# Two-stage attention with a gated convolution: groups of 508 tokens with their own halo, h summed on VectorE, outputs partly from float16 halves

## The chip, the cores and the metric

The kernel runs on one core of one Trainium2 chip. The metric is the time of one execution on the device, in microseconds (us). The kernel before took 354.98 us, the median of three runs (354.09 to 355.49). The profile comes from one further execution of the same kernel.

## What is computed

There are 4 batches of 12800 tokens with 128 channels, and 32 inducing vectors. In short:

```python
def mab(q, kv):                        # attention with kv as keys and as values
    s = scale * (q @ kv.transpose(0, 2, 1))
    a = np.exp(s - s.max(-1, keepdims=True))
    a /= a.sum(-1, keepdims=True) + 1e-09
    return a @ kv
h = mab(I, x)                          # 32 rows per batch: the inducing vectors attend to all tokens
y = mab(x, h)                          # every token attends to the 32 rows of h
# then, on y, a gate from a causal convolution over 5 tokens, per channel:
gate = 1 / (1 + np.exp(-sum(conv_w[k] * y_padded[:, k:k + S, :] for k in range(5))))
out = (gate * (y @ w_val)) @ w_out
```

The host transposes: the kernel gets x twice, as `xT` (batch, 128 channels, tokens) and as `xk` (batch, 128 rows, blocks, 128 channels), and writes the output transposed.

## The kernel before

Each batch is cut into seven units. Six are big: four groups (G = 4) of 512 tokens, one group for each quarter of the 128 partitions in the attention steps. One is small, four groups of 128 tokens; it stands first in batch 0 and last in the others (`units`, L29).

**Stage 1** makes h. For each unit `load_t` (L218) brings xT, 128 rows of 8192 bytes for a big unit, and `load_k` (L223) brings xk, which is the same tokens again with the token on the partition: 128 rows of 16 blocks of 512 bytes. Both are issued on SyncE's queue (SP), in the order xT, xk, xT, xk. `a_mm` (L229) makes the scores, `a_max` and `a_exp` (L238, L242) the exponentials, `a_tr` (L248) transposes them in blocks of 128 tokens on TensorE, `a_ev` (L254) copies them to SBUF, `a_h` (L259) multiplies them with xk, and `a_hev` (L268) copies the unit's sum. `a_h` is the only reader of xk.

**Between the stages**, once per batch, the `p_` functions (L274 to L381) join the units: `p_F` (L304) makes seven scaled diagonal matrices, `p_h` (L316) sums the seven units with seven float32 matmuls, `p_hq` (L323) normalizes h, and `p_v`, `p_w`, `p_wt`, `p_we` fold h into the weights of the convolution and of `w_val`, as pairs of float16 numbers (a high part and a rest).

**Stage 2** goes over the same units with the xT that is still in SBUF. `b_mm` to `b_back` (L384 to L426) make the attention weights of each token, `b_hi` (L429) and `b_lo` (L434) split them into two float16 halves; `b_lo` also copies, on GpSimd (POOL), the four tokens before each group, the halo, from the group or the unit in front. `c_gate` (L456) runs the five taps as 60 matmuls of 32 rows into four PSUM banks (tag `g`), `c_tanh` (L461) reads them, `c_val` (L466) fills a new tile of the same four banks, `c_gv` (L470) multiplies the two, `c_out` (L475) multiplies one group with `w_out` in float32, `c_ev` (L480) copies the result to SBUF, and after the fourth group the output leaves by a DMA on ScalarE's queue.

**The order** is made by a planner that runs while the program is built (`Plan`, L53). Every step is a task with an engine, a cost, a key (its due time, in units of stage 2), the tasks that it needs and the buffer that it takes. The planner plays the tasks through; of those that can start, an engine takes the one with the lowest key. The order of start becomes the order of the instructions on every engine, and the engines then keep to it. Stage 1 of batch b + 1 has keys in the middle of stage 2 of batch b, so both stages run side by side except in batch 0's stage 1 and in batch 3's stage 2.

Buffers limit how far ahead loads run: 12 for xT (held from the load to `b_mm` in stage 2), 4 for xk (held to `a_h`); the eight PSUM banks are `g` 4, `o` 2, `s` 1, `x` 1 (L38). The host builds `xk` in `kernel` (L607 to L612).

Of the kernel before, what the change touches and what calls it, by code (L numbers as in the profile page):

```python
# [24 lines left out]
SP = 16384.0  # L25
TINY = 1e-30


def units(b):  # L29
    small = [(0, 128)] if b == 0 else [(12288, 128)]  # L30
    big = [(2048 * u + 512 * (b == 0), 512) for u in range(6)]
    return small + big if b == 0 else big + small

# [4 lines left out]
BUFS = dict(xT=12, xk=4, E=2, ET=2, q=3, m=2, z=2, p=2, hl=3, gt=4, os=2, hs=1, nm=3, wst=2, wst2=2, gsc=2, hq=2, s=1, x=1, o=2, g=1)  # L38
LAT = 0.15
SLACK = 0.1  # L40
OUTK = 1.4
KA, KB, KP, KS = -2.5, 0.6, 4.0, 1.3
# [9 lines left out]

class Plan:  # L53
# [5 lines left out]
    def add(self, eng, dur, key, fn, args=(), deps=(), alloc=None, uses=(), lat=LAT):  # L59
        t = dict(i=len(self.tasks), eng=eng, dur=dur, key=key, fn=fn, args=args, deps=set(deps) | set(uses), alloc=alloc,  # L60
                 users=[], lat=lat, start=None, end=None)
# [71 lines left out]
def tile_kernel(ctx: ExitStack, tc: tile.TileContext, xT, xk, inducing, w_val, conv_w, w_out, out):  # L133
# [21 lines left out]
    def constants():  # L155
# [10 lines left out]
        V.memset(ones, 1.0)  # L166
        id4 = const.tile([P, M], F32, name="id4")
# [50 lines left out]
    def load_t(b, u):  # L218
        t0, w = units(b)[u]
        x = st[b, u, "xT"] = sbt("xT", [P, G * 512])  # L220
        nc.sync.dma_start(x[:, :G * w], xT[b, :, t0:t0 + G * w])

    def load_k(b, u):  # L223
        t0, w = units(b)[u]
        n = G * w // P
        x = st[b, u, "xk"] = sbt("xk", [P, 16, P])
        nc.sync.dma_start(x[:, :n, :], xk[b, :, t0 // P:t0 // P + n, :])

    def a_mm(b, u):  # L229
# [5 lines left out]
        for g in range(G):  # L235
            T.matmul(sc[M * g:M * g + M, :w], c_["iw"], x[:, w * g:w * g + w], start=True, stop=True, tile_position=(0, M * g))  # L236
# [11 lines left out]
    def a_tr(b, u):  # L248
        w = units(b)[u][1]
        et = st[b, u, "etp"] = ps("et", "x", [P, 4, P])  # L250
        for i in range(w // P):
            T.transpose(et[:, i, :], st[b, u, "E"][:, P * i:P * i + P], c_["identf"])  # L252

    def a_ev(b, u):  # L254
        n = units(b)[u][1] // P
        et = st[b, u, "et"] = sbt("ET", [P, 4, P])
        S.copy(et[:, :n, :], st[b, u, "etp"][:, :n, :])  # L257

    def a_h(b, u):  # L259
        n = units(b)[u][1] // P  # L260
        hp = st[b, u, "h"] = ps("h", "x", [P, 512])
        et, x = st[b, u, "et"], st[b, u, "xk"]
        for i in range(n):
            for g in range(G):
                T.matmul(hp[M * g:M * g + M, :P], et[:, i, M * g:M * g + M], x[:, n * g + i, :],  # L265
# [38 lines left out]
    def p_F(b):  # L304
        d = bat[b]
        f = d["f"]
        F = d["F"] = sbt("F", [P, NU, M])
        V.tensor_tensor(F, c_["id4"].rearrange("p (o q) -> p o q", o=1).broadcast_to([P, NU, M]), f.broadcast_to([P, NU, M]), ALU.mult)
# [6 lines left out]

    def p_h(b):  # L316
# [3 lines left out]
        for u in range(NU):  # L320
            T.matmul(t[:, :M], d["hs"][:, u, :], d["F"][:, u, :], start=u == 0, stop=u == NU - 1)  # L321
# [16 lines left out]
    def p_w(b):  # L338
# [10 lines left out]
        V.tensor_scalar(vmx, vmx, TINY, 1.0 / SW, ALU.max, ALU.mult)  # L349
# [16 lines left out]
        wo = d["wo"] = sbt("wo", [P, P], tag="wst")  # L366
        V.tensor_scalar(wo, c_["w2"], vmx, 0.5 / SP, ALU.mult, ALU.mult)

# [15 lines left out]
    def b_mm(b, u):  # L384
# [3 lines left out]
        for g in range(G):  # L388
            T.matmul(sc[M * g:M * g + M, :w], bat[b]["hq"], x[:, w * g:w * g + w], start=True, stop=True, tile_position=(0, M * g))  # L389

    def b_tr(b, u):
        w = units(b)[u][1]
# [3 lines left out]
    def b_max(b, u):  # L396
        n = units(b)[u][1] // M
# [3 lines left out]
    def b_sub(b, u):  # L401
        n = units(b)[u][1] // M
# [3 lines left out]
    def b_exp(b, u):  # L406
        n = units(b)[u][1] // M
# [3 lines left out]
    def b_sum(b, u):  # L411
        n = units(b)[u][1] // M
        z = st[b, u, "z"] = sbt("z", [P, 16, 1])
        V.tensor_reduce(z[:, :n, 0], st[b, u, "q"][:, :n, :], AX.X, ALU.add)
        V.tensor_scalar(z[:, :n], z[:, :n], 1e-9, 1.0 / SP, ALU.add, ALU.mult)
        V.reciprocal(z[:, :n], z[:, :n])  # L416

    def b_norm(b, u):
        n = units(b)[u][1] // M
# [3 lines left out]
    def b_back(b, u):  # L423
        w = units(b)[u][1]
# [4 lines left out]
    def b_hi(b, u):  # L429
        w = units(b)[u][1]  # L430
        h = st[b, u, "hl"] = sbt("hl", [P, 2, 520], F16)
        S.copy(h[:, 0, 4:4 + w], st[b, u, "p"][:, :w])  # L432

    def b_lo(b, u):  # L434
        w = units(b)[u][1]
        h = st[b, u, "hl"]
        Gp.tensor_tensor(h[:, 1, 4:4 + w], st[b, u, "p"][:, :w], h[:, 0, 4:4 + w], ALU.subtract)  # L437
        if u == 0:
            Gp.memset(h[:M, :, 0:4], 0.0)
        else:  # L440
# [6 lines left out]
    def strips(b, u, bank, d, k, first, last):  # L447
        w = units(b)[u][1]
        h, wst = st[b, u, "hl"], bat[b]["wst"]
        for i, (part, wp) in enumerate(((0, 0), (0, 1), (1, 0))):  # L450
            for g in range(G):
                s = slice(M * g, M * g + M)
                T.matmul(bank[:, g, :w], wst[s, wp, k, :], h[s, part, 4 - d:4 - d + w],  # L453
# [12 lines left out]
    def c_val(b, u):  # L466
        bank = st[b, u, "v"] = ps("v", "g", [P, G, 512])
        strips(b, u, bank, 0, TAPS, True, True)

    def c_gv(b, u, i):  # L470
        w = units(b)[u][1]
        t = st[b, u, i, "t"]
        V.scalar_tensor_tensor(t[:, :, :w], t[:, :, :w], 1.0, st[b, u, "v"][:, 2 * i:2 * i + 2, :w], ALU.add, ALU.mult)  # L473

    def c_out(b, u, g):  # L475
        w = units(b)[u][1]
        op = st[b, u, g, "o"] = ps("o", "o", [P, 512])
        T.matmul(op[:, :w], bat[b]["wo"], st[b, u, g // 2, "t"][:, g % 2, :w], start=True, stop=True)  # L478

    def c_ev(b, u, g):  # L480
# [4 lines left out]
        S.copy(os[:, w * g:w * g + w], st[b, u, g, "o"][:, :w])  # L485
# [16 lines left out]
    hl = {}  # L502
    hq = [None] * B
    ph = []
    wready = [None] * B

# [120 lines left out]
```

## Time and profile before

| | us |
|---|---|
| median of three runs | 354.98 |
| profiled execution, its own time | 354.44 |
| its span, first to last instruction | 352.7 |
| TensorE matmuls busy in it | 315.0 |
| VectorE busy | 197.9 |
| ScalarE busy | 176.0 |
| GpSimd busy | 103.3 |

The span lies 1.74 us below the execution's own time. Engines: PE is TensorE's matmuls and PEld its weight loads, DVE is VectorE, ACT ScalarE, POOL GpSimd, SP SyncE; a q behind a name is the engine's sequencer or queue. The profile's page shows the span in 40 slices, a digit for the busy tenths of each; the views of groups show a line of the kernel, the engine, the operation, output<-input with shapes, the count, and then the busy time, the mean length of one, and the idle time just before with what ended it.

### The profile page before, as it was taken

The numbers are of one execution on the slowest core, as the hardware profiler recorded it, in microseconds if no ns is written. First come the engines' busy times: TensorE is split into PE (matmuls) and PEld (weight loads), VectorE is DVE, ScalarE is ACT, GpSimd is POOL, SyncE is SP. The second block draws the span as 40 slices with busy tenths as digits, with TensorE's granted clock in tenths as the row PEclk, the third lists the DMA queues.
The fourth block names the chain that finished last, engine by engine and source line by source line (L and its number), as shares of the span: only waits on it lengthen the run. The fifth ranks groups of instructions, "written<-read, shape, count | busy, mean of one in ns | idle before, by whom it ended". The sixth has DMA issues, their size and how long they took to land.

```text
span 352.7 us, 8776 instructions
## 1 busy us (share of the span) xinstructions
PE 315.0 (89%) x3722; PEld 139.3 (39%) x3722; DVE 197.9 (56%) x415; ACT 176.0 (50%) x314; POOL 103.3 (29%) x202
## 2 busy tenths in 40 slices
PE   2475698989999999999999999999999999887774
PEld 0333455543343454343353444443354333332332
DVE  1432356656579773664678563666667758722220
ACT  1223313556553647466553557465654555624443
POOL 0000003434531443144431123443451457721000
PEclk9989959999999999999999999999999999989999
DMA  7999999838983293698983394012223230232233
GB/s 306 419 419 413 419 415 421 315 159 326 388 360 121 70 391 120 227 336 302 414 354 123 106 390 164 32 62 103 93 106 122 121 124 26 119 121 121 119 121 150
DMA packets 12481, 79.49 MB, mean 225 GB/s; under 512 B 1397, under 2 KB 1690, under 8 KB 3226
## 3 DMA queue, kind: packets, MB, share of 16 engines
q1 hardware_dynamic: 8064, 52.43, 38.2%
q10 hardware_dynamic: 4378, 26.50, 18.4%
q8 instruction: 29, 0.48, 0.6%
q14 instruction: 10, 0.08, 0.1%
HBM read 52.71 MB, written 26.21 MB: 224 GB/s over the span
## 4 chain that ended last, share of the span: by engine, by line
PE 79%; ACT 7%; DMA 7%; DVE 5%; issue 1%; ACTq 0%; SPq 0%; DVEq 0%
PE o L478 25%; PE g L453 24%; PE s L389 7%; PE s L236 6%; PE h L265 6%; PE v L453 4%; DMA xT<-in_xt_dram 4%; PE et L252 3%; ACT gt L464 3%; DMA raw<-in_moe_w_out_dram 3%; DVE gt L473 2%; PE t L321 2%; ACT os L485 2%; ACT E L246 1%; DVE nm L240 1%
## 5 line engine op out<-in xcount | busy, mean ns | idle before, releaser
L478 PE MATMUL o<-gt,wo 128*128 128x512 f32 (+1 forms) x224 | 105.0, 584 | 9.1 <-DVE gt L473 8.5
L453 PE MATMUL g<-hl,wstk 32*128 32x512 f16 (+1 forms) x1680 | 86.3, 352 | 0.0
L485 ACT COPY os<-o 128x512 f32<-128x512 f32 (+1 forms) x112 | 58.9, 542 | 50.6 <-PE o L478 49.9
L473 DVE SCALAR_TENSOR_TENSOR gt<-gt,v 128x1024 f32<-128x1024 f32 (+1 forms) x56 | 59.5, 1103 | 41.8 <-ACT os L485 30.1
L453 PEld LDWEIGHTS <-wstk 32*128 32x128 f16 x2016 | 44.7, 92 | 75.2 <-issue 19.3
L464 ACT ACTIVATE gt<-g,gsc 128x1024 f32<-128x1024 f32 (+1 forms) x56 | 54.4, 1019 | 35.0 <-PE g L453 26.8
L478 PEld LDWEIGHTS o<-gt,wo 128*128 128x128 f32 x224 | 36.1, 190 | 53.0 <-issue 32.7
L404 POOL TENSOR_TENSOR q<-q,m 128x512 f32<-128x512 f32 (+1 forms) x28 | 26.7, 955 | 103.2 <-DVE m L399 102.3
L421 POOL TENSOR_TENSOR q<-q,z 128x512 f32<-128x512 f32 (+1 forms) x28 | 26.7, 954 | 70.0 <-DVE z L416 50.6
L437 POOL TENSOR_TENSOR hl<-p,hl 128x512 f16<-128x512 f32 (+1 forms) x28 | 29.6, 1057 | 39.0 <-ACT hl L432 38.8
L246 ACT ACTIVATE E<-s,nm 128x512 f32<-128x512 f32 (+1 forms) x28 | 18.0, 643 | 34.8 <-DVE nm L240 27.1
L265 PE MATMUL h<-xk,ET 128*32 128x128 f32 x800 | 29.7, 289 | 2.5 <-ACT ET L257 2.5
L236 PE MATMUL s<-xT,iw 128*32 128x512 f32 (+1 forms) x224 | 30.7, 624 | 0.6 <-DMA xT<-in_xt_dram 0.3
L240 DVE TENSOR_REDUCE nm<-s 128x1 f32<-128x512 f32 (+1 forms) x28 | 17.6, 630 | 24.3 <-PE s L236 24.1
L265 PEld LDWEIGHTS h<-xk,ET 128*32 128x32 f32 x800 | 23.0, 117 | 17.6 <-ACT ET L257 10.6
L252 PE MATMUL et<-identf,E 128*128 128x128 f32 x100 | 18.1, 303 | 12.8 <-ACT E L246 12.0
L432 ACT CAST hl<-p 128x512 f16<-128x512 f32 (+1 forms) x28 | 16.1, 575 | 26.4 <-DVE p L426 25.1
L389 PE MATMUL s<-xT,hq 128*32 128x512 f32 (+1 forms) x224 | 27.6, 562 | 1.0 <-DVE q L394 1.0
L394 DVE STREAM_TRANSPOSE q<-s 128x512 f32<-128x512 f32 (+1 forms) x28 | 18.1, 645 | 13.3 <-PE s L389 13.2
L426 DVE STREAM_TRANSPOSE p<-q 128x512 f32<-128x512 f32 (+1 forms) x28 | 17.9, 646 | 11.9 <-POOL q L421 10.7
L453 PE MATMUL v<-hl,wstk 32*128 32x512 f16 (+1 forms) x336 | 21.2, 354 | 1.9 <-ACT gt L464 1.9
L409 ACT ACTIVATE q<-q 128x512 f32<-128x512 f32 (+1 forms) x28 | 16.4, 589 | 13.0 <-POOL q L404 12.5
(85 smaller groups left out, 194.8 us busy)
## 6 DMA issues: line engine op xcount, KB each, us to landing
xT<-in_xt_dram SPq DMA_DIRECT2D x24, 1024.0 KB, 9.5
xk<-in_xk_dram SPq DMA_DIRECT2D x24, 1024.0 KB, 11.4
out_dram<-os ACTq DMA_DIRECT2D x24, 1024.0 KB, 4.5
xT<-in_xt_dram SPq DMA_DIRECT2D x4, 256.0 KB, 8.7
xk<-in_xk_dram SPq DMA_DIRECT2D x4, 256.0 KB, 6.3
out_dram<-os ACTq DMA_DIRECT2D x4, 256.0 KB, 2.0
raw<-in_moe_w_val_dram ACTq DMA_DIRECT2D x1, 128.0 KB, 7.6
raw<-in_moe_w_out_dram ACTq DMA_DIRECT2D x1, 128.0 KB, 10.1
```

The costliest lines, as they stand in the source:

```text
L236: T.matmul(sc[M * g:M * g + M, :w], c_["iw"], x[:, w * g:w * g + w], start=True, stop=True, tile_position=(0, M * g))
L252: T.transpose(et[:, i, :], st[b, u, "E"][:, P * i:P * i + P], c_["identf"])
L265: T.matmul(hp[M * g:M * g + M, :P], et[:, i, M * g:M * g + M], x[:, n * g + i, :], start=i == 0, stop=i == n - 1, tile_position=(0, M * g))
L389: T.matmul(sc[M * g:M * g + M, :w], bat[b]["hq"], x[:, w * g:w * g + w], start=True, stop=True, tile_position=(0, M * g))
L404: Gp.tensor_tensor(q[:, :n], q[:, :n], st[b, u, "m"][:, :n].broadcast_to([P, n, M]), ALU.subtract)
L421: Gp.tensor_tensor(q[:, :n], q[:, :n], st[b, u, "z"][:, :n].broadcast_to([P, n, M]), ALU.mult)
L437: Gp.tensor_tensor(h[:, 1, 4:4 + w], st[b, u, "p"][:, :w], h[:, 0, 4:4 + w], ALU.subtract)
L453: T.matmul(bank[:, g, :w], wst[s, wp, k, :], h[s, part, 4 - d:4 - d + w], start=first and i == 0, stop=last and i == 2, tile_position=(M * ...
L464: S.activation(t[:, :, :w], st[b, u, "g"][:, 2 * i:2 * i + 2, :w], AF.Tanh, scale=bat[b]["gsc"])
L473: V.scalar_tensor_tensor(t[:, :, :w], t[:, :, :w], 1.0, st[b, u, "v"][:, 2 * i:2 * i + 2, :w], ALU.add, ALU.mult)
L478: T.matmul(op[:, :w], bat[b]["wo"], st[b, u, g // 2, "t"][:, g % 2, :w], start=True, stop=True)
L485: S.copy(os[:, w * g:w * g + w], st[b, u, g, "o"][:, :w])
```

## The change

The tokens are cut differently. A big unit is now four groups of 508 tokens, a small one four groups of 152. In stage 2 every group works on 512 (160) tokens: its own and the 4 (8) before it, read again from xT, which for this is loaded with 8 more tokens in front (`PAD`). So `b_lo` copies no halo. In stage 1 the blocks of tokens are 127 (76) long in place of 128: 16 (8) blocks per unit, and xk is loaded on 127 (76) partitions. xT has 11 buffers in place of 12.

The sum over units, h, is made by seven VectorE instructions (`p_hs`), followed by one matmul in place of seven. `c_val` writes into the gate's own PSUM tile, in batch 3 in two halves. `w_out` is scaled per output channel (`p_o1` to `p_o5`, with two transposes on TensorE) and kept as two float16 matrices, and in batches 0 to 2 also as float32. For the groups that `HALVES` names (two of four in batches 0 to 2, all four in batch 3) the product of gate and value is split into float16 halves, the high one by VectorE (`c_gh`) and the rest by GpSimd (`c_gl`), and `c_out` is three float16 matmuls in place of one float32 one. `c_ev` multiplies by the channel's scale. The planner has new keys per function and new costs.

```diff
 def units(b):
-    small = [(0, 128)] if b == 0 else [(12288, 128)]
-    big = [(2048 * u + 512 * (b == 0), 512) for u in range(6)]
+    small = [(0, 152)] if b == 0 else [(12192, 152)]
+    big = [(2032 * u + 608 * (b == 0), 508) for u in range(6)]
...
+def halo(w):
+    return 4 if w == 508 else 8
...
+def block(w):
+    return 127 if w == 508 else 76
+
+def blocks(b, u):
+    return sum(G * w // block(w) for _, w in units(b)[:u])
...
-KA, KB, KP, KS = -2.5, 0.6, 4.0, 1.3
+KA, KB, KP, KS = -3.17, 0.49, 3.18, 1.48
...
+def NVAL(b):
+    return 2 if b == 3 else 1
+
+def HALVES(b, i):
+    return b == 3 or i == 0
...
     def load_t(b, u):
         t0, w = units(b)[u]
-        x = st[b, u, "xT"] = sbt("xT", [P, G * 512])
-        nc.sync.dma_start(x[:, :G * w], xT[b, :, t0:t0 + G * w])
+        x = st[b, u, "xT"] = sbt("xT", [P, 2048])
+        nc.sync.dma_start(x[:, :PAD + G * w], xT[b, :, t0:t0 + PAD + G * w])
 
     def load_k(b, u):
-        t0, w = units(b)[u]
-        n = G * w // P
+        w = units(b)[u][1]
+        k, n = block(w), G * w // block(w)
         x = st[b, u, "xk"] = sbt("xk", [P, 16, P])
-        nc.sync.dma_start(x[:, :n, :], xk[b, :, t0 // P:t0 // P + n, :])
+        nc.sync.dma_start(x[:k, :n, :], xk[b, :k, blocks(b, u):blocks(b, u) + n, :])
...
     def a_tr(b, u):
-        for i in range(w // P):
-            T.transpose(et[:, i, :], st[b, u, "E"][:, P * i:P * i + P], c_["identf"])
+        for i in range(w // k):
+            T.transpose(et[:k, i, :], st[b, u, "E"][:, k * i:k * i + k], c_["identf"])
...
-                T.matmul(hp[M * g:M * g + M, :P], et[:, i, M * g:M * g + M], x[:, n * g + i, :],
+                T.matmul(hp[M * g:M * g + M, :P], et[:k, i, M * g:M * g + M], x[:k, n * g + i, :],
...
+    def p_hs(b, i):
+        d = bat[b]
+        u = (i + 1) % NU if b == 0 else i
+        if i == 0:
+            d["ha"] = sbt("ha", [P, P])
+            V.tensor_scalar(d["ha"], d["hs"][:, u, :], d["f"][:, u], None, ALU.mult)
+        else:
+            V.scalar_tensor_tensor(d["ha"], d["hs"][:, u, :], d["f"][:, u], d["ha"], ALU.mult, ALU.add)
+
     def p_h(b):
...
-        for u in range(NU):
-            T.matmul(t[:, :M], d["hs"][:, u, :], d["F"][:, u, :], start=u == 0, stop=u == NU - 1)
+        T.matmul(t[:, :M], d["ha"], c_["id4"], start=True, stop=True)
...
-            T.matmul(sc[M * g:M * g + M, :w], bat[b]["hq"], x[:, w * g:w * g + w], start=True, stop=True, tile_position=(0, M * g))
+            o = PAD + w * g
+            T.matmul(sc[M * g:M * g + M, :wide(w)], bat[b]["hq"], x[:, o - halo(w):o + w], start=True, stop=True, tile_position=(0, M * g))
...
     def b_lo(b, u):
...
-            v = units(b)[u - 1][1]
-            Gp.tensor_copy(h[:M, :, 0:4], st[b, u - 1, "hl"][P - M:, :, v:4 + v])
-        for g in range(1, G):
-            Gp.tensor_copy(h[M * g:M * g + M, :, 0:4], h[M * g - M:M * g, :, w:4 + w])
...
+    def c_gh(b, u, i):
+        w = units(b)[u][1]
+        h = st[b, u, i, "gh"] = sbt("gh", [P, 2, 512], F16)
+        V.tensor_copy(h[:, :, :w], st[b, u, i, "t"][:, :, :w])
+
+    def c_gl(b, u, i):
+        w = units(b)[u][1]
+        l = st[b, u, i, "gl"] = sbt("gl", [P, 2, 512], F16)
+        Gp.tensor_tensor(l[:, :, :w], st[b, u, i, "t"][:, :, :w], st[b, u, i, "gh"][:, :, :w], ALU.subtract)
+
     def c_out(b, u, g):
         w = units(b)[u][1]
         op = st[b, u, g, "o"] = ps("o", "o", [P, 512])
-        T.matmul(op[:, :w], bat[b]["wo"], st[b, u, g // 2, "t"][:, g % 2, :w], start=True, stop=True)
+        if not HALVES(b, g // 2):
+            T.matmul(op[:, :w], bat[b]["wf32"], st[b, u, g // 2, "t"][:, g % 2, :w], start=True, stop=True)
+            return
+        wh = bat[b]["wh"]
+        for i, (x, k) in enumerate((("gh", 0), ("gh", 1), ("gl", 0))):
+            T.matmul(op[:, :w], wh[:, k, :], st[b, u, g // 2, x][:, g % 2, :w], start=i == 0, stop=i == 2)
...
-        S.copy(os[:, w * g:w * g + w], st[b, u, g, "o"][:, :w])
+        S.activation(os[:, w * g:w * g + w], st[b, u, g, "o"][:, :w], AF.Copy, scale=bat[b]["osc"])
...
-    xt = x.transpose(0, 2, 1)
-    xk = _np.empty((nb, P, NT // P, P), x.dtype)
+    xt = _np.zeros((nb, P, PAD + NT), x.dtype)
+    xt[:, :, PAD:] = x.transpose(0, 2, 1)
+    xk = _np.zeros((nb, P, blocks(0, NU), P), x.dtype)
     for b in range(nb):
-        for t0, w in units(b):
-            n = G * w // P
-            xk[b, :, t0 // P:t0 // P + n] = x[b, t0:t0 + G * w].reshape(n, P, P).transpose(1, 0, 2)
+        for u, (t0, w) in enumerate(units(b)):
+            k, n, o = block(w), G * w // block(w), blocks(b, u)
+            xk[b, :k, o:o + n] = x[b, t0:t0 + G * w].reshape(n, k, P).transpose(1, 0, 2)
```

More of the change, by code (lines that the diff above doesn't have):

```diff
@@ L560, in stage2 @@
             hi = add("ACT", l(w, 0.2, 0.6), key, b_hi, (b, u), uses=[bk], alloc="hl")
[L561 to L563 removed]
+            lo = add("POOL", l(w, 0.3, 1.18), key, b_lo, (b, u), uses=[bk, hi])
             key += KS
```

149 lines of the change are left out of this document (101 added, 48 removed).

## The prediction

> **What bounds the kernel now.** I read the page from the top (busy shares, slices, queues), then the DMA issues, the groups of instructions with shapes kept apart, and TensorE's timeline around the last loads.
>
> ```profile
> span 352.7 us, 8776 instructions
> ...
> PE 315.0 (89%) x3722; PEld 139.3 (39%) x3722; DVE 197.9 (56%) x415; ACT 176.0 (50%) x314; POOL 103.3 (29%) x202
> ...
> PE   2475698989999999999999999999999999887774
> ...
> DMA  7999999838983293698983394012223230232233
> GB/s 306 419 419 413 419 415 421 315 159 326 388 360 121 70 391 120 227 336 302 414 354 123 106 390 164 32 62 103 93 106 122 121 124 26 119 121 121 119 121 150
> DMA packets 12481, 79.49 MB, mean 225 GB/s; under 512 B 1397, under 2 KB 1690, under 8 KB 3226
> ...
> q1 hardware_dynamic: 8064, 52.43, 38.2%
> q10 hardware_dynamic: 4378, 26.50, 18.4%
> ```
>
> TensorE is the bound: 89% busy over all, 9 tenths or more from the tenth slice to the 34th. In the first eight slices the DMA engines are the bound (stage 1 of batch 0, up to 421 GB/s); in the last third their digits are 1 to 3. So a change to TensorE's work pays, and a change to the loads costs nothing, as long as they stay fast. The second condition is what I look at first, because the change touches every load of xk.
>
> **The loads.** The issues, from the view of DMAs:
>
> ```profile
> xT<-in_xt_dram SPq DMA_DIRECT2D x24, 1024.0 KB, 9.5
> xk<-in_xk_dram SPq DMA_DIRECT2D x24, 1024.0 KB, 11.4
> out_dram<-os ACTq DMA_DIRECT2D x24, 1024.0 KB, 4.5
> ...
> ind<-in_inducing_dram ACTq DMA_DIRECT2D x1, 16.0 KB, 4.6
> raw<-in_moe_conv_w_dram ACTq DMA_DIRECT2D x1, 5.0 KB
> ```
>
> How many of the 16 DMA engines share a transfer? The packets tell. A row of a transfer is a packet (8192 bytes in a big load), and each engine that took part ends with a packet of a few bytes. Queue q1 carries 56 loads of 128 rows: 8064 / 56 = 144 = 128 + 16, so 16 engines, 8 rows each. Queue q10 carries 30 transfers of 128 rows (28 outputs, two weights), 30 x 144 = 4320; the 16 KB of `ind` in 32 rows of 512 bytes, 32 + 16 = 48; that leaves 4378 - 4368 = 10 for `conv_w`, 5 KB in 5 rows: 5 + 5, so 5 engines. The 1397 packets under 512 bytes say the same: 86 x 16 + 16 + 5. Every transfer here is cut into equal shares of rows: 8, 2, 1.
>
> The big load of xk will have 127 rows, and 127 is prime: no two or more engines up to 16 can have equal shares. **Two readings** fit the rows. Equal shares only: then one engine carries all 127 rows. Shares rounded up: then 16 engines take 8 rows or 7, and nothing changes. I take the first, because every one of the 88 transfers has equal shares and none shows a remainder being handled; nothing in this trace excludes the second. The Trainium skill, "DMA: Bandwidth & Descriptors", section "Why a DMA increments its semaphore by 16 and not by 1", states the first: the engine count is the largest number up to 16 that divides the slowest dimension of both sides, and it names 127 partitions as running on 1. By that rule the sum is the one below; the 5 ends of `conv_w` agree with it, and no run here shows a prime number of rows above 16.
>
> What one engine does: the best slice moves 421 GB/s, 26.3 GB/s for each of 16, or 311 ns for a packet of 8192 bytes. From the other side, q1's packets took 38.2% of 16 x 352.7 us for 52.43 MB, which is 337 ns for 8192 bytes, waits included. I take 311 (the stretch in which the engines had nothing to wait for) and keep 337 for the range. In the order of the code, on the engine that carries xk:
>
> - big xk: 127 x 311 ns = 39.5 us each, before 8 x 311 = 2.5; 24 of them: 949
> - small xk, 76 rows of 4096 bytes: four equal shares of 19 rows, 3.0 us each; three before the last big one: 9
> - this engine's sixteenth of the xT loads: 8 x 8160 bytes, 2.5 us, 24 of them, and three small ones of 0.7: 62
> - its sixteenth of the outputs of two batches and two units, 2 x 15.6 + 2 x 2.5: 36
>
> Sum 1056. The first bytes move at 2.4 us (slice one has 306 of 419 GB/s). All loads stand in one queue, so they follow each other on that engine as long as SP has issued the next one. It has: four buffers of xk leave three loads, 120 us, queued. One gap I see: an xT load for the first unit of batch 2 waits for the fifth `b_mm` of batch 0 (11 buffers), and in the order of now that stands just behind the last `a_h`:
>
> ```profile
> 228.35 1.06 PE L389 MATMUL s<-xT,hq 128*32 128x512 f32 x8
> ...
> 231.16 1.08 PE L265 MATMUL h<-xk,ET 128*32 128x128 f32 x32
> ...
> 238.72 0.42 PE L265 MATMUL h<-xk,ET 128*32 128x128 f32 x8
> 238.96 1.04 PE L389 MATMUL s<-xT,hq 128*32 128x512 f32 x8
> ...
> 323.59 3.42 PE L453 MATMUL g<-hl,wstk 32*128 32x512 f16 x60
> ...
> 329.23 0.83 PE L453 MATMUL v<-hl,wstk 32*128 32x512 f16 x12 [0.31 <-ACT gt L464]
> ...
> 333.43 3.42 PE L453 MATMUL g<-hl,wstk 32*128 32x512 f16 x60
> ```
>
> That is 7.8 us after the last big `a_h`, once: 7. The last big load lands at 1056 + 2.4 + 7 = **1065 us**.
>
> **What is left then.** TensorE keeps its order, so it stands at that `a_h`, with all that the planner put behind it still to do. Now that is 352.7 - 231.2 = 121.5 us: four big units of stage 2 of batch 2, and batch 3. What the change makes of it, and of the rest, comes from the groups:
>
> ```profile
> L478 PE MATMUL o<-gt,wo 128*128 128x512 f32 x192 | 99.0, 630 | 7.9 <-DVE gt L473 7.4 <-ACT E L246 0.5
> L453 PE MATMUL g<-hl,wstk 32*128 32x512 f16 x1440 | 82.2, 375 | 0.0
> L473 DVE SCALAR_TENSOR_TENSOR gt<-gt,v 128x1024 f32<-128x1024 f32 x48 | 56.5, 1217 | 36.4 <-ACT os L485 25.6 <-PE v L453 8.9 <-ACT hl L432 1.5
> L485 ACT COPY os<-o 128x512 f32<-128x512 f32 x96 | 55.1, 588 | 45.0 <-PE o L478 44.3
> L464 ACT ACTIVATE gt<-g,gsc 128x1024 f32<-128x1024 f32 x48 | 50.9, 1110 | 33.2 <-PE g L453 25.1 <-DMA out_dram<-os 7.6 <-ACT os L485 0.4
> ...
> L437 POOL TENSOR_TENSOR hl<-p,hl 128x512 f16<-128x512 f32 x24 | 27.9, 1162 | 28.9 <-ACT hl L432 28.9
> ...
> L404 POOL TENSOR_TENSOR q<-q,m 128x512 f32<-128x512 f32 x24 | 25.1, 1048 | 45.8 <-DVE m L399 44.9 <-PE o L478 0.2
> ...
> L252 PE MATMUL et<-identf,E 128*128 128x128 f32 x100 | 18.1, 303 | 12.8 <-ACT E L246 12.0 <-DVE gt L473 0.5 <-DVE hs L271 0.3
> ...
> L271 DVE COPY hs<-h 128x128 f32<-128x128 f32 x28 | 7.9, 283 | 20.0 <-PE h L265 20.0
> ...
> L321 PE MATMUL t<-F,hs 128*128 128x32 f32 x56 | 7.5, 289 | 0.0
> ...
> L362 DVE CAST wr<-wf 128x768 f16<-128x768 f32 x4 | 2.2, 560 | 0.1
> ```
>
> - **Outputs.** A float32 `c_out` is 99.0 / 96 = 1.03 us. Three float16 passes over 508 columns are not in the trace. Nearest: the gate's 60 matmuls, four side by side, take 3.42 us in the timeline, 228 ns a pass, so 0.69. Other end: each pass at half a float32 `c_out` (two records), 1.55, a loss of 0.52. I take 0.69: the type decides, and it is the row of that type. Saved 0.34 each: 0.7 us a unit in batches 0 to 2, 1.4 in batch 3.
> - **The halves.** `c_gh` by the cast of 768 elements in 560 ns: 0.74 us; `c_gl` by POOL's 1162 ns for 512: 2.3 us. It waits for `c_gh`; behind it on POOL stand the next unit's two steps of the softmax, and DVE waits for those. In batch 3 POOL then has 2 x 1.05 + 1.16 + 2 x 2.3 = 7.9 us a unit.
> - **Batch 3's period** is 9.84 us (the gate at 333.43, one before at 323.59). TensorE would need 3.42 + 0.83 + 1.06 + 4 x 0.69 = 8.1; the chain through the gate's banks 3.4 + 2 x 1.1 + 0.4 + 1.2 and four handovers, 8; POOL 7.9. So 8.3, limited by all three: 1.5 saved a unit.
> - **h.** Each batch loses six of seven L321 matmuls, 7.5 / 4 x 6 / 7 = 1.6 us of TensorE, and gets two transposes of 0.30 for `w_out` and seven DVE steps of about 0.28 (as L271): the path between the stages keeps its length, within 1 us either way.
> - **Halo, widths, scale.** The halo's copies leave POOL, which is idle 71% of the span: nothing on the path. 508 columns for 512, 152 for 128: under 1% of TensorE, both signs. `c_ev` with a scale costs between nothing (588 ns now) and 0.1 us (an activation of twice the size takes 1110), under an ACT that is half idle.
>
> From the 121.5: four units of 0.7, six of 1.5, 1.0 for h, makes 13; the last unit pays 2 more for `c_gh` and `c_gl` ahead of its outputs. So 111. Everything else of the edits lies under the loads, since a unit's work (315 us of TensorE over some 25 units, 12.6) fits three times into a load.
>
> **Forecast**: 1065 + 111 = 1176 of span, and 1.7 around it (354.44 against 352.7): **1178 us**. The profiled 354.44 is 0.5 below the median of 354.98, nothing beside this.
>
> **The rivals.**
>
> A, the other side: the second reading holds, 16 engines share 127 rows, and the loads stay hidden. Then TensorE stays the bound: 60 float16 outputs of big units in place of float32 at 0.34 are 20, h gives 4, batch 3's chain 3 more beside its outputs, the last unit costs 2. 354.4 - 25 = 329. For it: nothing in the rows forbids unequal shares. Against it: none of the 88 transfers shows one. It decides at one point, the number of engines for 127 rows; already with four engines a load of xk takes 9.9 us and, with xT, 24 of them 298, so that the end would come near 450.
>
> The SBUF rule speaks against A's gain. The Trainium skill, "SBUF — State Buffer", section "Who interferes with whom", says that a VectorE copy in a two-port mode and a GpSimd instruction block each other. By it POOL would wait up to 2 x 0.74 us a unit in batch 3 and A would come out near 338; no row here shows such a pair.
>
> B: one engine, but not back to back, or at the slow end. At 337 ns a packet the 24 loads take 79 us more; a gap of 3 us at each load, because an issue waits for the buffer of the load that has just landed, 72 more. 1250 to 1330. For it: SP waits 81.6 us in the trace for `a_h` to free xk's buffers; against: three loads are queued.
>
> ```profile
> SPq L227 <- PE h L265: 81.6, 12, 23.8
> ```
>
> C: shares rounded up, and the gain lost: POOL's halves arrive late, with only two output banks, and the last stage runs at 10 us a unit: 350 to 358.
>
> **Numbers.** Forecast 0.75, B 0.08, A 0.14, C 0.03. Packets 2% faster or 4% slower than 311 ns (towards the 337) move the forecast by -20 to +38 us, the place of the last `a_h` in the new order (one unit earlier or later) by 10 each way, further gaps by up to 40: 1130 to 1250. With B, 1110 to 1310; A and C, 17 in 100, lie outside, and a range down to them would say nothing. A measurement of this kernel can tell about 0.5% from no change. Faster: A and a little of C, 0.15; the same: 0.01; slower: 0.84.
>
> **What would show it.** Packets under 512 bytes: 1397 - 24 x 15 - 4 x 12 = 989, and q1 at 24 x (144 + 128) + 4 x (144 + 80) = 7424. The DMA digits at 0 or 1 in most slices (one engine of 16), some 67 GB/s on average, TensorE near 25% busy, the chain of waits almost all DMA on xk, and `a_h` (L265) in steps of some 42 us. The groups of L478's successor would show 0.69 us an output, POOL's new group 2.3 us. I am wrong if xk still lands some 11 us after its issue: then A or C holds, and the number of small packets says so at once.

## The result, and the profile after

The changed kernel takes **1225.8 us** (median of four runs, 1219.99 to 1226.64), the kernel before beside it 355.24 (four runs, 354.09 to 357.09): 3.446 times as long, with a 95% interval of 3.427 to 3.464. Ratios and their intervals, here and below, leave out runs that came out over 1.5% above the fastest of the same kernel; medians and ranges are over all runs. The forecast was 1178, the range 1110 to 1310. The profiled execution took 1226.03 us, with a span of 1224.1.

These lines of the changed kernel's page answer to those of before. The two rows of tenths are the busy share of TensorE and of the 16 DMA engines in 40 slices, and PEclk is the granted clock.

```profile
span 1224.1 us, 8946 instructions
...
PE 364.5 (30%) x3788; PEld 156.0 (13%) x3788; DVE 258.3 (21%) x506; ACT 186.2 (15%) x314; POOL 151.7 (12%) x129
...
PE   1101110120210220160462230161633220259886
...
PEclk9996555555665665575676665576866665568979
DMA  2011111111101110202122201221312201101222
...
DMA packets 11842, 79.62 MB, mean 65 GB/s; under 512 B 989, under 2 KB 1282, under 8 KB 8754
...
q1 hardware_dynamic: 7424, 52.55, 11.9%
...
another core or an unknown queue 64%; PE 24%; DVE 4%; DMA 4%; ACT 2%; issue 1%; POOL 0%; ACTq 0%; SPq 0%; DVEq 0%; POOLq 0%
```

The same bytes move at 65 GB/s in place of 225, and the DMA digit stands at 0 or 1 in 26 of the 40 slices: about one engine of 16 works. The packet counts are those that the forecast worked out for one engine, 989 and 7424, to the last packet. The chain of waits does not name its main link (64% is put down to "an unknown queue"); the view of waits does, as time, number and longest:

```profile
DVE nm L279 <- PE s L275: 527.8, 21, 42.8
...
PE s L275 <- DMA xT<-in_xt_dram: 422.8, 19, 39.8
...
PE h L307 <- DMA xk<-in_xk_dram: 281.8, 8, 36.6
```

TensorE waits for loads 27 times here, up to 40 us each: mostly for xT, which stands behind an xk load in the same queue, and for xk itself. All the rest waits for TensorE. SyncE's queue shows the rhythm (start, length, then the instruction that issues a load):

```profile
25.43 40.14 SPq L260 DMA_DIRECT2D xT<-in_xt_dram  x1
65.62 3.00 SPq L266 DMA_DIRECT2D xk<-in_xk_dram  x1
68.67 39.59 SPq L260 DMA_DIRECT2D xT<-in_xt_dram  x1
108.30 2.91 SPq L266 DMA_DIRECT2D xk<-in_xk_dram  x1
...
1017.85 40.67 SPq L260 DMA_DIRECT2D xT<-in_xt_dram  x1
```

A pair of loads passes every 43 us. By the packet records, the 24 big loads of xk take 40.5 to 48.2 us each (41.2 at the median; a packet takes 313 ns), with 2.45 us between them (xT's share on this engine), or 6.22 where the loads of a small unit stand between, and the last one ends 1084.3 us into the span. What stands behind it is in TensorE's timeline (start, length, and in brackets the idle time before and its releaser):

```profile
1085.67 0.74 PE L275 MATMUL s<-xT,iw 128*32 128x152 f32 x8 [35.57 <-DMA xT<-in_xt_dram]
...
1090.25 1.27 PE L307 MATMUL h<-xk,ET 127*32 127x128 f32 x32
...
1092.32 3.40 PE L532 MATMUL g<-hl,wstk 32*128 32x508 f16 x60
...
1142.03 3.40 PE L532 MATMUL g<-hl,wstk 32*128 32x508 f16 x60
1152.46 4.89 PE L532 MATMUL g<-hl,wstk 32*128 32x508 f16 x60
1165.24 3.64 PE L532 MATMUL g<-hl,wstk 32*128 32x508 f16 x60
...
1189.93 3.40 PE L532 MATMUL g<-hl,wstk 32*128 32x508 f16 x60
1199.93 3.40 PE L532 MATMUL g<-hl,wstk 32*128 32x508 f16 x60
```

From 1085.7 to the end there are 138.4 us; the forecast had 111. The units left are the ones that it counted, but batch 3 (from 1142.03) runs at 10.0 to 12.8 us a unit, not at 8.3. TensorE did not stand at the last big `a_h` either, but ahead of it, at the small unit's `a_mm`, whose xT lands just behind that xk; the `a_h` follows at 1090.25.

Two questions are left for the experiments: is it the 127 rows, and by which rule; and what does the rest of the change do, which the loads cover here?

### The profile page after: what moved, and what is told of

It reads as the page before. It is cut to its first block, busy times and chain, and to the rows that moved or that the text cites. A ratio compares the mean times of both kernels' runs of the same rounds, so it can differ in the third digit from the quotient of the medians.

```text
span 1224.1 us, 8946 instructions
## 1 busy us (share of the span) xinstructions
PE 364.5 (30%) x3788; PEld 156.0 (13%) x3788; DVE 258.3 (21%) x506; ACT 186.2 (15%) x314; POOL 151.7 (12%) x129
## 3 DMA queue, kind: packets, MB, share of 16 engines
q1 hardware_dynamic: 7424, 52.55, 11.9%
## 4 chain that ended last, share of the span: by engine, by line
another core or an unknown queue 64%; PE 24%; DVE 4%; DMA 4%; ACT 2%; issue 1%; POOL 0%; ACTq 0%; SPq 0%; DVEq 0%; POOLq 0%
PE g L532 8%; DMA xT<-in_xt_dram 4%; PE o L570 3%; PE h L307 3%; PE s L275 3%; PE o L574 3%; PE s L473 2%; PE et L292 1%; DVE gt L553 1%; ACT gt L543 1%; DVE ha L363 1%; ACT os L581 0%; DVE z L499 0%; DVE nm L279 0%
## 5 line engine op out<-in xcount | busy, mean ns | idle before, releaser
L275 PE MATMUL s<-xT,iw 128*32 128x508 f32 (+1 forms) x224 | 43.3, 860 | 423.1 <-DMA xT<-in_xt_dram 422.8
L532 PE MATMUL g<-hl,wstk 32*128 32x508 f16 (+1 forms) x2016 | 123.3, 376 | 43.1 <-ACT gt L543 33.8
L307 PE MATMUL h<-xk,ET 127*32 127x128 f32 (+1 forms) x832 | 42.8, 368 | 306.2 <-DMA xk<-in_xk_dram 281.8
L581 ACT ACTIVATE os<-o,osc 128x508 f32<-128x508 f32 (+1 forms) x112 | 70.0, 642 | 166.8 <-PE o L570 96.1
L564 POOL TENSOR_TENSOR gl<-gt,gh 128x1016 f16<-128x1016 f32 (+1 forms) x35 | 67.8, 1939 | 222.2 <-DVE gh L559 219.2
L553 DVE SCALAR_TENSOR_TENSOR gt<-gt,g 128x1016 f32<-128x1016 f32 (+1 forms) x56 | 60.4, 1101 | 64.9 <-PE g L532 63.7
L307 PEld LDWEIGHTS h<-xk,ET 127*32 127x32 f32 (+1 forms) x832 | 32.2, 148 | 322.7 <-issue 290.5
L543 ACT ACTIVATE gt<-g,gsc 128x1016 f32<-128x1016 f32 (+1 forms) x56 | 55.2, 1020 | 73.5 <-PE g L532 41.8
L570 PE MATMUL o<-gt,wf 128*128 128x508 f32 (+1 forms) x84 | 48.4, 675 | 0.2 <-ACT os L581 0.2
L574 PE MATMUL o<-gh,wh 128*128 128x508 f16 (+1 forms) x140 | 44.1, 402 | 0.9 <-ACT os L581 0.8
L505 POOL TENSOR_TENSOR q<-q,z 128x512 f32<-128x512 f32 (+1 forms) x28 | 27.0, 964 | 115.4 <-DVE z L500 71.5
```

The costliest lines, as they stand in the source:

```text
L275: T.matmul(sc[M * g:M * g + M, :w], c_["iw"], x[:, PAD + w * g:PAD + w * g + w], start=True, stop=True, tile_position=(0, M * g))
L307: T.matmul(hp[M * g:M * g + M, :P], et[:k, i, M * g:M * g + M], x[:k, n * g + i, :], start=i == 0, stop=i == n - 1, tile_position=(0, M * g))
L532: T.matmul(bank[:, g, :w], wst[s, wp, k, :], h[s, part, halo(w) - d:halo(w) - d + w], start=first and i == 0, stop=last and i == 2, tile_p ...
L543: S.activation(t[:, :, :w], st[b, u, "g"][:, 2 * i:2 * i + 2, :w], AF.Tanh, scale=bat[b]["gsc"])
L564: Gp.tensor_tensor(l[:, :, :w], st[b, u, i, "t"][:, :, :w], st[b, u, i, "gh"][:, :, :w], ALU.subtract)
L570: T.matmul(op[:, :w], bat[b]["wf32"], st[b, u, g // 2, "t"][:, g % 2, :w], start=True, stop=True)
```

## The experiments

The kernel before was run again beside each group of experiments: 354.45 us (7 runs) beside those on the loads, 354.93 (13) beside val_whole, no_halves, z_one_input and cast_on_act, 353.68 (19) beside the last four. Ratios are to these. "Split" and "whole" below are `c_val` in two pieces or in one (`NVAL`), "halves" the float16 halves of the outputs (`HALVES`).

### The loads

**rows128**, the changed kernel with all 128 rows of xk loaded (the 128th row is not used):

```diff
-        nc.sync.dma_start(x[:k, :n, :], xk[b, :k, blocks(b, u):blocks(b, u) + n, :])
+        nc.sync.dma_start(x[:, :n, :], xk[b, :, blocks(b, u):blocks(b, u) + n, :])
```

> The changed kernel with one edit: each load of xk brings all 128 rows of the host's array (the last one, or the last 52 of a small unit, are zeros that nothing reads). Theory 1, one DMA engine carries a load of 127 rows: 16 engines again, 1397 packets under 512 bytes, TensorE the bound again, 335 to 345 us. Rival, the slowness comes from the blocks of 127 tokens or from rows at odd addresses: the time stays above 1000 us.

Measured: 370.85 us (369.66 to 373.35), ratio 1.049 (1.040 to 1.058). One row more, and 855 of the 871 us are gone. But the time is outside the 335 to 345 expected: the rest of the change is not worth the 25 us that rival A of the prediction gave it; it costs 16. From its page and DMA issues:

```profile
DMA packets 12482, 80.67 MB, mean 219 GB/s; under 512 B 1397, under 2 KB 1690, under 8 KB 9370
...
xk<-in_xk_dram SPq DMA_DIRECT2D x24, 1024.0 KB, 10.6
```

1397 small packets again, and xk lands 10.6 us after its issue.

**rows127_before**, the kernel before with each load of xk cut into rows 0 to 126 and row 127:

```diff
-        nc.sync.dma_start(x[:, :n, :], xk[b, :, t0 // P:t0 // P + n, :])
+        for r0, r1 in ((0, 127), (127, P)):
+            nc.sync.dma_start(x[r0:r1, :n, :], xk[b, r0:r1, t0 // P:t0 // P + n, :])
```

> The kernel before with one edit: each load of xk is two transfers, rows 0 to 126 and row 127. Theory 1: each part runs on one engine, 1397 - 28 x 14 = 1005 packets under 512 bytes, some 43.5 us for each big unit and 1200 to 1260 us in all. Rival (blocks or addresses, not the number of rows): 355 us and a few more for the additional issues.

Measured: 1241.24 us (one run), as theory 1 expected. Nothing but the cut of the loads makes the kernel before as slow as the changed one. Its small packets, 1005 of them as worked out:

```profile
DMA packets 12089, 79.49 MB, mean 64 GB/s; under 512 B 1005, under 2 KB 1298, under 8 KB 2834
```

**rows112_15** and **rows124_3**, the changed kernel with the 127 rows loaded in two pieces (the second in the same way with 124):

```diff
-        nc.sync.dma_start(x[:k, :n, :], xk[b, :k, blocks(b, u):blocks(b, u) + n, :])
+        for r0, r1 in (((0, 112), (112, 127)) if k == 127 else ((0, k),)):
+            nc.sync.dma_start(x[r0:r1, :n, :], xk[b, r0:r1, blocks(b, u):blocks(b, u) + n, :])
```

> The changed kernel with one edit: the 127 rows of a big xk load in two transfers, 112 rows and 15 rows. Theory 1: 16 and 15 engines, 1397 - 48 + 24 x 15 = 1709 packets under 512 bytes, the time of the run with 128 rows within 10 us. Rival: over 1000 us.

> The changed kernel with one edit: the 127 rows of a big xk load in two transfers, 124 rows and 3 rows. If the engines need equal shares, 124 = 4 x 31 gives 4 engines and 3 gives 3: 1397 - 48 - 24 x 9 = 1133 packets under 512 bytes, some 10 us of one engine for a load beside 2.5 for xT, 400 to 460 us. If only an odd or a prime number of rows is special and 124 is rounded up to 16 shares: 1397 - 48 + 24 x 3 = 1421 packets, and the time of the run with 128 rows.

Measured: 400.8 us (396.27, 405.34) for 112 + 15, and 526.7 (526.52, 526.87; ratio 1.486, 1.472 to 1.501) for 124 + 3. The lines of small packets, of rows112_15 and of rows124_3:

```profile
DMA packets 12562, 79.62 MB, mean 202 GB/s; under 512 B 1709, under 2 KB 2002, under 8 KB 9474
```

```profile
DMA packets 11986, 79.62 MB, mean 152 GB/s; under 512 B 1133, under 2 KB 1426, under 8 KB 8898
```

Both counts are those of equal shares: 112 rows on 16 engines and 15 on 15; 124 rows on 4 (31 each, though 16 engines could take 8 or 7) and 3 on 3. So these runs show one, three, four, 15 and 16 engines, and all fit one rule: **the transfer is cut into equal shares of its rows, and the number of engines is the largest up to 16 that divides them**. It is the rule of the Trainium skill, "DMA: Bandwidth & Descriptors", section "Why a DMA increments its semaphore by 16 and not by 1", which the prediction set beside the rows; these runs agree with it. They leave one gap: all row counts above 16 here (32, 76, 112, 124, 127, 128) go to 16, 4 or 1 engines, which the largest power of two up to 16 that divides them would give as well. Both times are outside what I had expected, on the slow side. In rows112_15 a 896 KB piece lands 17.8 us after its issue and the 120 KB piece after 19.7, against 10.6 for the whole 1024 KB in rows128: cutting one load into two costs 25 to 35 us here. It is not only the additional transfer: by the packet records a row of 8192 bytes of xk takes 499 ns at the median in rows112_15, and 309 in rows128; for xT's rows it is 455 and 308. Why the packets are slower, and why 124 + 3 takes 527 us where 313 ns a packet make 9.7 us a load, was not taken apart.

### What the rest of the change costs

rows128 is 16 us over the kernel before. All kernels below but the last load 128 rows, and so stand beside rows128.

**val_whole** makes `c_val` whole in batch 3 too; **no_halves** keeps the split and takes the halves out everywhere (all outputs by float32):

```diff
 def NVAL(b):
-    return 2 if b == 3 else 1
+    return 1
```

```diff
 def HALVES(b, i):
-    return b == 3 or i == 0
+    return False
```

> The run with 128 rows (370.85 us), and NVAL is 1 in every batch: the value's matmuls are not cut in two halves in batch 3. There each half takes 0.82 us, as long as the whole, and the second half waits for VectorE to have read the first. Theory 2, this chain through the gate's banks costs most of the 16 us over the kernel before: 0.8 + 0.3 us a unit and the clock that TensorE loses while it waits, 358 to 364 us. Rival, VectorE and GpSimd hold each other up in all batches: 366 to 369 us.

> The run with 128 rows (370.85 us), and no group has float16 halves: every c_out is one float32 matmul, c_gh and c_gl are gone. If TensorE's work sets the time, 60 outputs of 0.35 us more: 385 to 392 us. If the halves cost on VectorE and GpSimd what they save on TensorE: 366 to 374 us.

Measured: val_whole 358.32 us (354.57 to 360.48, ratio 1.017, 1.005 to 1.030), no_halves 351.44 (349.9 to 353.54, ratio 0.994, 0.990 to 0.999). Each takes out most of the 16 us or more. val_whole is where theory 2 put it; no_halves is faster than both of its expectations. Why the split is dear is in TensorE's timeline of batch 3, of rows128 first and then of val_whole:

```profile
308.71 3.77 PE L532 MATMUL g<-hl,wstk 32*128 32x508 f16 x60
...
314.70 0.82 PE L532 MATMUL g<-hl,wstk 32*128 32x508 f16 x6 [0.82 <-ACT gt L543]
316.89 1.45 PE L532 MATMUL g<-hl,wstk 32*128 32x508 f16 x6 [1.37 <-DVE gt L553]
318.27 1.03 PE L574 MATMUL o<-gh,wh 128*128 128x508 f16 x2
```

```profile
313.31 3.40 PE L532 MATMUL g<-hl,wstk 32*128 32x508 f16 x60 [1.39 <-DVE gt L553]
316.64 0.60 PE L574 MATMUL o<-gh,wh 128*128 128x508 f16 x2
...
318.98 0.82 PE L532 MATMUL g<-hl,wstk 32*128 32x508 f16 x12 [0.88 <-ACT gt L543]
...
322.31 1.04 PE L532 MATMUL g<-hl,wstk 32*128 32x508 f16 x16 [1.12 <-DVE gt L553]
```

Half of the value product, 6 matmuls in two of the four quarters of the array, takes 0.82 us, as long as the whole, 12 matmuls in four quarters. In rows128 the second half also stands behind a wait of 1.37 us for VectorE's `gt` (`c_gv`), and the planned order puts the outputs behind it. In the same stretch the granted clock is lower (0.87 from 285.5 to 353.6; 1.00 in val_whole from 282 to 345): an output's two matmuls take 1.03 and not 0.60. So the step from 308.71 to the next gate takes 12.2 us against 9.0: 1.45 for the second half, 1.2 for slower outputs, 0.4 for a slower gate, 0.2 for waits. Where the clock is whole (1.00 from 333.6 to 353.6) the step of rows128 is 10.0, so the split costs 1.0 there, and the rest goes with the lower clock. What lowers the clock is not shown. It can hardly be the sum of TensorE's idle time: in batch 3's big units the waits for `gt` come to 11.9 us in rows128 and to 10.7 in val_whole. Nor is it only how they lie: in rows128 both stand within 3 us with 0.82 us of work between them (in val_whole at least 2.2), but they do so in its steps at the whole clock too.

**z_one_input** and **cast_on_act** ask whether VectorE's waits for POOL are the cost: the first replaces the scalar_tensor_tensor of `b_sum` (16 elements a row, 215 ns at L415 before, where it had one input, 831 ns in rows128) by an operation with one input, the second makes `c_gh` on ScalarE in place of VectorE.

```diff
-        V.scalar_tensor_tensor(z[:, :n], z[:, :n], 1.0 / SP, c_["eps"][:, :n], ALU.mult, ALU.add)
+        V.tensor_scalar(z[:, :n], z[:, :n], 1.0 / SP, 1e-9 / SP, ALU.mult, ALU.add)
```

```diff
-        V.tensor_copy(h[:, :, :w], st[b, u, i, "t"][:, :, :w])
+        S.copy(h[:, :, :w], st[b, u, i, "t"][:, :, :w])
```

> The run with 128 rows (370.85 us), and b_sum scales its 16 sums with a tensor_scalar with two constants, as in the kernel before, in place of an operation that reads a second tensor from SBUF. Rival theory (the two engines hold each other up): VectorE's line falls from 836 ns to some 220 to 280, 17 us of VectorE in all, and the time by 4 to 10 us. Theory 2: VectorE's line falls the same, the time by 2 us at most.

> The run with 128 rows (370.85 us), and the high halves (c_gh) are cast by ScalarE at the same place of the order, not by VectorE. It takes 30 us from VectorE, casts of 2.33 us behind GpSimd among them, and gives some 36 us to ScalarE. Rival theory: 358 to 366 us. Theory 2: 368 to 376 us, as ScalarE's tanh stands on the chain of batch 3.

Measured: 370.5 us (366.44 to 373.14, ratio 1.046, 1.032 to 1.061) and 369.79 (368.37 to 375.68, ratio 1.047, 1.035 to 1.058). Neither differs from rows128 (1.049) by more than can be told; for the first both sides had expected the operation to fall to 220 to 280 ns. It stays at 831 ns with one input, in the groups of before, rows128 and z_one_input:

```profile
L415 DVE TENSOR_SCALAR z<-z 128x16 f32<-128x16 f32 x24 | 5.2, 215 | 0.8
```

```profile
L499 DVE SCALAR_TENSOR_TENSOR z<-z,eps 128x16 f32<-128x16 f32 x24 | 20.0, 831 | 0.8
```

```profile
L499 DVE TENSOR_SCALAR z<-z 128x16 f32<-128x16 f32 x24 | 19.9, 831 | 0.8
```

So the number of its inputs is not the reason. Where no tensor_tensor of POOL runs beside it, it takes 169 to 177 ns in all three kernels; where one does, it ends with that one, within 0.04 us. POOL's new step, `c_gl`, is the longest of them. In rows128 at 112 us, POOL and VectorE:

```profile
112.13 2.11 POOL L564 TENSOR_TENSOR gl<-gt,gh 128x1016 f16<-128x1016 f32 x1 [3.65 <-DVE gh L559]
```

```profile
112.61 1.66 DVE L499 SCALAR_TENSOR_TENSOR z<-z,eps 128x16 f32<-128x16 f32 x1
```

The 16 elements end just as POOL's 2.11 us end (114.27 and 114.24). The Trainium skill, "SBUF — State Buffer", section "Who interferes with whom", has VectorE and GpSimd lock each other out of a shared pair of ports: casts, copies and tensor_scalars can do so when their operands meet the page's conditions, and so do operations with two SBUF inputs beside a GpSimd operation that reads SBUF. This row and the replaced one agree with it. But the casts are not what the 16 us hang on: with 27 us of them taken off VectorE (230.8 us busy for 257.9) the time stays, though batches 0 to 2 are 2.4 us shorter in its profile (the table below).

**whole_no_halves**, **halves_b012** and **halves_b3** part the places of the halves. All have `c_val` whole in every batch; `HALVES` is as in the diff for the first, `b < 3 and i == 0` for the second and `b == 3` for the third:

```diff
-    return b == 3 or i == 0
+    return False
```

> 128-row loads of xk, the value product in one piece in every batch, float32 outputs everywhere (no float16 halves). Theory (the halves and the split value product are what costs beside the loads, and without halves the split costs nothing, since its two pieces of 6 matmuls stand back to back in no_halves): the same as no_halves, 351.4 us, within 3. Rival (the split costs its 0.8 us a unit wherever it stands): 6 units by 0.8 less, 346 to 347.

> 128-row loads, value product in one piece, float16 halves of two groups in batches 0 to 2 only; batch 3 with float32 outputs. Theory (the halves cost in batches 0 to 2, where VectorE is over 80% busy and waits for POOL): 355 to 359 us, near val_whole's 358.3. Rival (they cost in batch 3 and at the tail): 350 to 353, near no_halves' 351.4.

> 128-row loads, value product in one piece, float16 halves only in batch 3. Theory (the halves cost in batches 0 to 2): 350 to 353 us, near no_halves' 351.4. Rival (they cost in batch 3 and at the tail): 355 to 359, near val_whole's 358.3.

Measured: whole_no_halves 356.51 us (352.4 to 358.6, ratio 1.006, 1.001 to 1.011), halves_b012 355.94 (355.67 to 358.31, ratio 1.011, 1.002 to 1.021), halves_b3 351.09 (350.82 to 353.06, ratio 0.994, 0.991 to 0.998). The last two are where the theory put them. The first is a miss for both sides: without halves the split does not cost nothing, and not 0.8 us a unit either; it gains. The timelines show it, of whole_no_halves first and then of no_halves:

```profile
311.50 3.40 PE L532 MATMUL g<-hl,wstk 32*128 32x508 f16 x60
...
317.11 0.82 PE L532 MATMUL g<-hl,wstk 32*128 32x508 f16 x12 [0.31 <-ACT gt L543]
319.41 1.94 PE L570 MATMUL o<-gt,wf 128*128 128x508 f32 x4 [1.48 <-DVE gt L553]
321.28 3.40 PE L532 MATMUL g<-hl,wstk 32*128 32x508 f16 x60
```

```profile
311.46 3.40 PE L532 MATMUL g<-hl,wstk 32*128 32x508 f16 x60
...
317.07 0.84 PE L532 MATMUL g<-hl,wstk 32*128 32x508 f16 x12 [0.31 <-ACT gt L543]
317.83 1.12 PE L570 MATMUL o<-gt,wf 128*128 128x508 f32 x2
319.40 1.09 PE L570 MATMUL o<-gt,wf 128*128 128x508 f32 x2 [0.45 <-DVE gt L553]
320.43 3.40 PE L532 MATMUL g<-hl,wstk 32*128 32x508 f16 x60
```

With the split as the planner orders it there, the two halves run back to back and one pair of outputs goes into the wait for `c_gv`, so 0.45 us of idle time is left of 1.48. A row of the profiled executions for each kernel shows all of it. The columns are: the first gate of the kernel (end of batch 0's stage 1), the stretch from there to batch 3's first big gate, the stretch from that gate to the end of the span, and the usual step from one of batch 3's gates to the next.

| kernel | c_val in batch 3 | halves in batches 0-2 / 3 | median us | first gate | batches 0-2 | batch 3 | step |
|---|---|---|---|---|---|---|---|
| before | whole | no / no | 354 | 60.4 | 220.8 | 71.5 | 9.8 |
| rows128 | split | yes / yes | 370.9 | 57.7 | 227.8 | 82.3 | 10.0-12.9 |
| cast_on_act | split | yes / yes | 369.8 | 59.2 | 225.4 | 81.9 | 9.9-12.6 |
| val_whole | whole | yes / yes | 358.3 | 57.2 | 227.4 | 68.2 | 9.0 |
| halves_b012 | whole | yes / no | 355.9 | 57.1 | 227.4 | 69.6 | 9.8 |
| halves_b3 | whole | no / yes | 351.1 | 57.3 | 223.8 | 68.2 | 9.0 |
| whole_no_halves | whole | no / no | 356.5 | 57.6 | 224.0 | 70.3 | 9.8 |
| no_halves | split | no / no | 351.4 | 59.0 | 223.8 | 66.8 | 9.0 |

The two stretches repeat better than the medians: between kernels that have the same code there, to 0.4 us in batches 0 to 2 (cast_on_act aside) and to 0.7 in batch 3. The plan is made anew for each kernel, so a price is that of an edit with the order that it brings. Three prices can be read off:

- The halves in batches 0 to 2 cost 3.6 us (227.4 against 223.8), although they save TensorE work: over this stretch it is busy for 216.4 us in halves_b012 and for 220.3 in halves_b3, 3.9 less, but its idle time is 7.5 longer. VectorE's busy time goes from 155.76 to 183.61 of 225 us, as the view of stretches has it for halves_b3 and then halves_b012 (the same window for both, in which halves_b012 is 3.4 us behind at the end):

```profile
57.00:282.00 225.00, 221.55 (x2707) 95.89 (x2707) 155.76 (x341) 136.65 (x227) 71.29 (x72) 1.00 0.58 220
```

```profile
57.00:282.00 225.00, 214.05 (x2707) 92.72 (x2703) 183.61 (x355) 131.38 (x221) 105.63 (x90) 0.98 0.56 216
```

More than half of the additional idle time is one wait, for the sum of h that the change put on VectorE (`p_hs`, tile `ha`): 5.0 us with halves (val_whole) and 1.0 without (no_halves), time, number and longest. What makes `ha` late is not shown; with the casts on ScalarE (cast_on_act) the wait stays at 5.1 us.

```profile
PE t L369 <- DVE ha L363: 5.0, 3, 2.0
```

```profile
PE t L369 <- DVE ha L363: 1.0, 1, 1.0
```

- In batch 3 the halves gain 0.8 us a unit over whole float32 outputs, and the split with float32 outputs gains as much. A step of 9.0 is reached either way, and nothing here goes below it.
- Both together, as in the change, cost 14 us in batch 3 against the halves alone (82.3 against 68.2).

The other edits (no halo on POOL, h on VectorE, scaled `w_out`) are left as 3.0 us in batches 0 to 2 (223.8 against 220.8), about paid back ahead of the first gate; they were not taken apart. halves_b3 and no_halves beat the kernel before by 0.6%, hardly more than can be told.

**one_engine_whole** goes back to the loads of the change, 127 rows, with `c_val` whole and no halves (the two edits of val_whole and no_halves):

> The changed kernel with its 127-row loads, the value product in one piece and no float16 halves. Theory (the last load lands when it did, 1086 us into the span, and the 138 us behind it are longer than the forecast's 111 because of the split value product and the halves): 138 falls to about 115, the time to 1195 to 1205 us. Rival (the work behind the last load is long for another reason, the 508-column steps or h on VectorE): within 8 us of 1226.

Measured: 1212.95 us (1212.65, 1213.26; ratio 3.439, 3.403 to 3.475), between what the theory and the rival expected.

```profile
1087.12 0.74 PE L275 MATMUL s<-xT,iw 128*32 128x152 f32 x8 [33.55 <-DMA xT<-in_xt_dram]
1087.63 1.94 PE L307 MATMUL h<-xk,ET 127*32 127x128 f32 x32
...
1139.55 3.40 PE L532 MATMUL g<-hl,wstk 32*128 32x508 f16 x60
```

TensorE goes on at the same place within 1.5 us, and to the end of the span (1211.5) 124.4 us follow in place of 138.4. So 14 of the 27 us that the forecast lacked there are the split and the halves together. In three parts, before from its last big `a_h` (231.2) and the others from where TensorE goes on, with the forecast as the 121.5 us of before less its own savings:

| us | before | forecast | changed | one_engine_whole |
|---|---|---|---|---|
| to batch 3's first gate | 50.0 | 46.2 | 56.4 | 52.4 |
| batch 3's six big units | 62.1 | 53.1 | 67.9 | 62.3 |
| from the last small unit's gate to the end | 9.4 | 11.4 | 14.2 | 9.6 |

Without split and halves, batch 3 and the end take what they took before; of the 13 us that the forecast lacks even there, 10.5 are what it had taken off, for cheaper outputs above all, and 2.4 stand ahead of batch 3.

## Why the prediction was right

Point by point, by its own steps.

- **One engine for 127 rows** (first reading): right, and it is the whole result. rows128 takes the loads out and 855 of the 871 us go; rows127_before adds them alone and comes out at 1241. The count of packets that the prediction gave as its sign came out exactly. The case for the first reading was 88 transfers with equal shares and none with a remainder; 124 + 3 now shows it for a number with several divisors.
- **The last big load lands at 1065**: it was 1084.3, and TensorE went on at 1085.7. The packet was priced well: where nothing disturbs them, packets start 311 ns apart, as forecast. The working lacked what slows them: while the other 15 engines move their shares of the next xT, three to six packets of xk take up to 690 ns, some 28 us over the 24 loads, and some 5 us go by beside packets of the queue for instructions (q8 on the page). It had too much for the outputs (36, some 31 moved) and for the gap of 7 us behind the fifth `b_mm`, which did not appear. That 33 us too few and 12 too many cancel in part is luck. "SP has issued the next one" held, though not with three loads queued. Rival B's gap at each load did not come.
- **111 us behind it**: it was 138. The mis-sized term is "batch 3's period", 8.3 and "limited by all three": its six units took 67.9 us and not 53.1, 15 of the 27. Another 10 lie ahead of batch 3 and 3 in the last unit (the table above), 4.6 of them between 1085.7 and the last big `a_h`, which the forecast had first. The outputs were priced well: 0.65 us each in the timeline at full clock, forecast 0.69. So was POOL's `c_gl`, 2.1 for 2.3. `c_gh` was 0.68 us alone and 0.90 on average for 0.74, since some stand beside POOL's step. What the working lacked is the split of `c_val`, which the diff shows and the sum gave no price: 0.82 us for each half, and a granted clock that is lower beside it. And the gate's own chain (the 60 matmuls, tanh, value product, `c_gv`, 9.0 us with its handovers in val_whole and halves_b3) was put at 8, so that there was less to gain than I had counted even where the order is good.
- **1.0 us saved for h**: not seen. In the changed kernel TensorE waits 6.4 us for `ha`, four times and up to 2.0, about the 1.6 a batch that its matmuls no longer take.
- **"Everything else of the edits lies under the loads"**: right for the time, as the whole distance is loads and what follows them. But the reasoning behind rival A, that TensorE's saved work is saved time, was wrong: rows128 is A's kernel, and took 370.9 us, not 329, nor the 338 with waits between VectorE and POOL. Had A's reading held, the sign of the answer would have been wrong.
- **"No row here shows such a pair"** (VectorE held up by POOL) was a misreading: in the trace of before, L415's small operation takes 448 to 977 ns five times and 170 to 176 otherwise, each time ending with a step of POOL.
- The errors of the two terms, +20.7 to 1085.7 and +27.4 behind it, have the same sign and make the 48 us between 1178 and 1225.8.

## What to carry to other kernels

Before changing the shape of a transfer, factor its number of rows: in these runs the largest divisor up to 16 is the number of engines, and the packet counts in the profile of a kernel that runs already can be read for it. A padded row that nobody reads was worth 855 us here, while cutting the load into 112 + 15 rows still cost 25 to 35. Where work is taken from the engine that is busiest, ask in each stage whether its busy time or a chain through a few banks sets the step: here 3.9 us less of TensorE's work in batches 0 to 2 went with 3.6 us more time, as TensorE waited longer, mostly for VectorE between the stages.

## What the runs showed of the hardware

- SyncE's issuing instruction itself is held: an xT load's issue takes 40 us (L260 in the fence of SyncE's queue) while one engine still has the last xk load's packets to move; before, an issue took 0.3 to 1.4 us. I had counted three loads as standing in the queue.
- Six matmuls in two quarters of the array take 0.82 us, as long as twelve in four. To work on half of the quarters saves nothing here.
- Two transfers of 112 and 15 rows take longer to land (17.8 and 19.7 us) than one of 128 rows with nearly as many bytes (10.6), and a packet of 8192 bytes takes 499 ns at the median in place of 309.
- On the one engine that carries xk, packets of 8192 bytes start 311 ns apart, and take up to 690 ns while the other 15 engines move the next load.
- An operation of VectorE on 16 elements a row takes 169 to 177 ns, and up to 1.69 us beside a step of POOL, with which it ends.
